# One out run per pair of heads, and half an out unit carried over a stage: attention followed by a two-layer snake network on one core

## The chip, the cores and the metric

The kernel runs on one core of a Trainium2 chip. The metric is the device time of one execution in microseconds (us). Each kernel has one profile. All runs here are with a mean granted TensorE clock of 0.985 to 0.996. Engines: PE is TensorE's matmul work, PEld its weight loads, ACT is ScalarE, DVE VectorE, POOL GpSimd.

## The reference, cut to what matters

```python
# 8 batches, 12 heads, 448 tokens, head size 64
q_n, k_n = rmsnorm(q, g_q), rmsnorm(k, g_k)
attn = softmax(q_n @ k_n.T / sqrt(64))
x = (attn @ v)            # per batch 448 x 768
h = x @ w_in              # 768 -> 2048, the "first product"
g = h + sin(alpha * h) ** 2 / (alpha + 1e-9)
out = g @ w_out           # 2048 -> 768, the "second product" or "out work"
```

## The kernel before

The program is a row of stages on TensorE: attention of batch 0, first product of batch 0, then for each batch b from 1 to 7 an attention stage followed by a first product. The second product of batch b-1 is cut into small steps of two matmuls each, called fillers, that are dealt out between the score and value matmuls of the attention of batch b. They give TensorE work while ACT computes exponentials. The second product of batch 7 stands alone at the end.

448 tokens are three tiles of 128 and a rest of 64. So even batches have three out units of 128 tokens, and odd batches have four: the fourth joins the rest of the even batch before and the first 64 tokens of the odd one. A unit has 16 steps (batch 0 has half units of 8 steps, because the second half of `w_out` lands late: in the trace it is issued at 47.4 us, the two halves take 26.6 and 29.2 us from issue to landing, and the first out matmul starts at 66.5). An attention stage therefore holds 48 or 64 steps, in turn.

```python
psum = ctx.enter_context(tc.tile_pool(name="ps", bufs=4, space=bass.MemoryType.PSUM))  # 4 slots, each a bank_pair
...
def scores(pi, t, warm=0):          # one tile of 128 keys, two heads
    sc = bank_pair("sc")
    ...                             # two matmuls, each on 64 rows of the array
    nc.scalar.activation(expT[pi][:, 2 * t:2 * t + 2, :], sc[:, :, :S], ACT.Exp, scale=SCALE)
...
units = [(i, (0, 1)) for i in range(NT + odd)] if b else [(i, (h,)) for h in range(2) for i in range(NT)]
if b == B - 1:
    units[-1:] = [(NT + odd - 1, (h,)) for h in range(2)]
...
for b in range(1, B):
    fillers.extend(second_product(b - 1))
    n_fill = len(fillers)
    ...
    step_of(ci, 5)()                # rsqrt of the norm for pairs 4 and 5: two small ACT instructions
    ...
    for p in range(NP):             # six pairs of heads
        ...                         # quota: 16 steps for pair 0, the rest spread evenly; part = its quarters
        if p == 0 and b > 1:
            fill(part[2])
        scores(pi, 0)
        scores(pi, 1)
        if p:
            attend(pi - 1)          # av: 16 value matmuls, then logarithm, exponential, multiply
        else:
            fill(part[3] - (part[2] if b > 1 else 0))
        if p % 2 == 0:
            rest_scores(pi)         # the rest keys of two pairs
        beside_e(4 * p)             # norm of the next batch; holds an rsqrt on ACT in pairs 2 and 4
        if p:
            fill(part[2])
            beside_e(4 * p + 1)
            scores(pi, 2)
            fill(part[3] - part[2])
        else:
            beside_e(4 * p + 1)
            scores(pi, 2)
        beside_e(4 * p + 2)
        fill(part[4] - part[3])
        beside_e(4 * p + 3)
    fill(len(fillers))
    attend(b * NP + NP - 1)
    ...
    first_product(b, beside_h(b))
```

Of the kernel before, what the change touches and what calls it, by code (L numbers as in the profile page):

```python
# [32 lines left out]
def kernel(  # L33
# [21 lines left out]
    B, H, S, D = q.shape  # L55
# [4 lines left out]
    MT = D_FF // P  # L60
    NP = H // 2
    NT = S // P
# [24 lines left out]
    def bank_pair(name):  # L87
        return psum.tile([P, 2, 512], F32, tag="ps", name=name)
# [3 lines left out]
    def load_qk(ci, k_queue=nc.sync):  # L92

        b, dp = ci // NC, ci % NC
        qk[ci] = inp.tile([P, 2, 2 * NJ, D], F32, tag="qk", name="qk")
        for which, src, queue in ((0, q, nc.sync), (1, k, k_queue)):
            heads = src[b].rearrange("(hi dp pp) (p j) d -> dp (pp p) hi (j d)", hi=2, pp=2, j=NJ)[dp]
            queue.dma_start(out=qk[ci][:, which].rearrange("p (hi j) d -> p hi (j d)", hi=2), in_=heads)

    def rest_rows(pi, hi):  # L100

        r = (hi + pi) % 2
        return slice(r * 64, r * 64 + 64)

    def load_v(b):


        vb[b] = vpool.tile([P, NT * H + NP, D], BF16, tag="vb", name="vb")
        parts = []
        tok = v[b].rearrange("h (p j) d -> p h (j d)", j=NJ)  # L110
        for jj in range(2):
            parts.append((vb[b][jj * 64:jj * 64 + 64, :NT * H, :].rearrange("p (h t) d -> p h (t d)", t=NT),
                          tok[:, :, jj * NT * D:(jj + 1) * NT * D]))
        last = v[b].rearrange("(hi dp pp) (p j) d -> j hi pp p dp d", hi=2, pp=2, j=NJ)[NJ - 1]
        slots = vb[b][:, NT * H:, :].rearrange("p (dp pp) d -> pp p dp d", pp=2)
        for hi in range(2):
            for pp in range(2):
                parts.append((slots[pp][rest_rows(pp, hi)], last[hi, pp]))
        return [lambda o=o, i=i: nc.gpsimd.dma_start(out=o, in_=i) for o, i in parts]  # L119
# [147 lines left out]
    def scores(pi, t, warm=0):  # L267

        sc = bank_pair("sc")
        for _ in range(warm):  # L270
            nc.tensor.matmul(sc[:, 0], blank[:, :P], blank, start=True, stop=True)
        qt, kt = qkT[pi][:, 0, :], qkT[pi][:, 1, :]
        if pi not in expT:
            expT[pi] = epool.tile([P, 2 * NT + 1, S], BF16, tag="expT", name="expT")
        for hi in range(2):
            r = slice(hi * 64, hi * 64 + 64)
            nc.tensor.matmul(sc[:, hi, :S], kt[r, t * P:(t + 1) * P], qt[r, :], start=True, stop=True)  # L277
        nc.scalar.activation(expT[pi][:, 2 * t:2 * t + 2, :], sc[:, :, :S], ACT.Exp, scale=SCALE)  # L278

    def rest_scores(pi):  # L280

        sc = bank_pair("sc3")
        for pp in range(2):
            if pi + pp not in expT:
                expT[pi + pp] = epool.tile([P, 2 * NT + 1, S], BF16, tag="expT", name="expT")
            for hi in range(2):
                r = slice(hi * 64, hi * 64 + 64)
                nc.tensor.matmul(sc[rest_rows(pp, hi), pp, :S], qkT[pi + pp][r, 1, NT * P:S], qkT[pi + pp][r, 0, :],
                                 start=True, stop=True)
        for pp in range(2):  # L290
            nc.scalar.activation(expT[pi + pp][:, 2 * NT, :], sc[:, pp, :S], ACT.Exp, scale=SCALE)  # L291
# [72 lines left out]
    def second_product(b):  # L364


        steps = []
        odd = b % 2
        rows = [out[c * S:(c + 1) * S, :].rearrange("(p j) d -> j p d", j=NJ) for c in range(B)]
        units = [(i, (0, 1)) for i in range(NT + odd)] if b else [(i, (h,)) for h in range(2) for i in range(NT)]  # L370
        if b == B - 1:
            units[-1:] = [(NT + odd - 1, (h,)) for h in range(2)]
        for i, halves in units:
            st = {}

            def step(m, i=i, halves=halves, st=st):
                if m == 0:
                    st["ps"] = bank_pair("ops")
                c0 = odd * (S + REST) + i * P if i < NT else NT * P
                lhsT = g_sb[:, m, c0:c0 + P]  # L380
                for k, half in enumerate(halves):
                    nc.tensor.matmul(st["ps"][:, k, :HALF], lhsT, w_out_sb[:, m, half * HALF:(half + 1) * HALF],  # L382
                                     start=(m == 0), stop=(m == MT - 1))
                if m == MT - 1:
                    n = len(halves)
                    osb = opool.tile([P, 2, HALF], F32, tag="osb", name="osb")
                    nc.vector.tensor_copy(osb[:, :n], st["ps"][:, :n, :HALF])  # L387
                    o = osb[:, :n].rearrange("p a d -> p (a d)")
                    cols = slice(halves[0] * HALF, (halves[-1] + 1) * HALF)
                    for jj in range(2):  # L390
                        dst = rows[b][odd + 2 * i + jj] if i < NT else rows[b - 1 + jj][(NJ - 1) * (1 - jj)]
                        eng = nc.scalar if b == B - 1 and jj else nc.sync
                        eng.dma_start(out=dst[:, cols], in_=o[jj * 64:jj * 64 + 64, :])
            each = 2 // len(halves)
            steps += [lambda m=m, s=step, e=each: [s(m * e + x) for x in range(e)] for m in range(MT // each)]
        return steps

    fillers = deque()

    def fill(n):  # L400
        for _ in range(min(n, len(fillers))):
            fillers.popleft()()
# [29 lines left out]
    def begin_norm(ci):  # L432
        norm[ci] = norm_tasks(ci)
        if ci + 2 < NC * B and ci != NC + 2:
            load_qk(ci + 2)

    def step_of(ci, *steps):
        return lambda: [norm[ci].steps[n]() for n in steps]

    def beside_h(b):  # L440

        ci = NC * b + 5
        if ci >= NC * B:
            return {}
        return {0: [lambda: begin_norm(ci)], 1: [step_of(ci, 0)], 3: [step_of(ci, 1)], 4: [step_of(ci, 3)],
                5: [step_of(ci, 2)], 7: [step_of(ci, 4)]}

    FIRST = 16
    for p in range(NP):
        scores(p, 0, BUSY[2 + p])  # L450
        scores(p, 1)
# [39 lines left out]

    for b in range(1, B):
        nc.scalar.preload_act_table_set(EXP_LN)
        fillers.extend(second_product(b - 1))
        n_fill = len(fillers)

        at = [[] for _ in range(4 * NP + 8)]
        s0, ci = 2, NC * b + 2
        if b == 1:
            load_qk(ci + 2)  # L500
        step_of(ci, 5)()
        at[s0].append(step_of(ci, 6))
        if b + 1 < B:
            for ci in (NC * b + 3, NC * b + 4):
                at[s0] += [lambda ci=ci: begin_norm(ci), step_of(ci, 0, 1, 2)]
                for n, step in ((4, 3), (5, 4), (6, 5), (8, 6)):
                    at[s0 + n].append(step_of(ci, step))
                s0 += 8
            for n, part in enumerate(load_v(b + 1)):
                at[s0 - 1 + n].append(part)  # L510

        def beside_e(slot):
            for task in at[slot]:
                task()

        for p in range(NP):
            pi = b * NP + p
            if p == 0:
                quota = min(FIRST, n_fill)
            else:  # L520
                left = max(n_fill - FIRST, 0)
                quota = left * p // (NP - 1) - left * (p - 1) // (NP - 1)
            part = [quota * j // 4 for j in range(5)]
# [5 lines that stand above are left out]
                attend(pi - 1)  # L529
            else:  # L530
                fill(part[3] - (part[2] if b > 1 else 0))
            if p % 2 == 0:
                rest_scores(pi)
            beside_e(4 * p)
            if p:
                fill(part[2])
                beside_e(4 * p + 1)
                scores(pi, 2)
                fill(part[3] - part[2])
            else:  # L540
                beside_e(4 * p + 1)
                scores(pi, 2)
            beside_e(4 * p + 2)
            fill(part[4] - part[3])
            beside_e(4 * p + 3)
        fill(len(fillers))
        attend(b * NP + NP - 1)
        for slot in range(4 * NP, len(at)):
            beside_e(slot)
        first_product(b, beside_h(b))  # L550
# [30 lines left out]
```

## Time and profile before

| | before |
|---|---|
| median of four runs | 465.85 us (465.0 to 466.45) |
| span of the profiled run | 463.9 us |
| PE / ACT / POOL / DVE busy | 441.4 / 344.2 / 293.3 / 227.2 us |
| attention stage with 64 steps (batches 2, 4, 6) | 37.60 us |
| attention stage with 48 steps (batches 3, 5) | 33.12 us |
| the same, batch 1 and batch 7 | 34.43 and 32.46 us |
| first product, each | 18.28 us |

A stage's length is read from the chain of waits, where each first product shows as one piece of 96 matmuls: the start of the next piece less the start of this one, less 18.28. Three of these pieces (start, duration; 155.31 - 99.43 - 18.28 = 37.60, and 206.71 - 155.31 - 18.28 = 33.12):

```profile
99.43 18.28 PE hps L341 x96
155.31 18.28 PE hps L341 x96
206.71 18.28 PE hps L341 x96
```

### The profile page before, as it was taken

What the parts mean: (1) busy time and instruction counts of PE and PEld (TensorE: products, weight loads), DVE (VectorE), ACT (ScalarE), POOL (GpSimd) and SP (SyncE); (2) the same over time, 40 slices, a digit from 0 to 9 for tenths busy, and PEclk for the clock granted to TensorE, in tenths of its full rate; (3) what the DMA queues carried; (4) which work ended last, traced back from release to release, by engine and by line L of the source; (5) the groups of instructions that cost most, each with busy time, mean ns of one, the idle gap of its engine ahead of it and who ended that gap; (6) DMA issues with size and microseconds to landing.
All of it is one profiled execution on the core that took longest, in us unless ns stands there. A gap on an engine that the chain in (4) does not pass through costs nothing.

```text
span 463.9 us, 7776 instructions
## 1 busy us (share of the span) xinstructions
PE 441.4 (95%) x2956; PEld 213.7 (46%) x2956; DVE 227.2 (49%) x331; ACT 344.2 (74%) x555; POOL 293.3 (63%) x299
## 2 busy tenths in 40 slices
PE   7678999999999999999999999999999999999996
PEld 2323544445444454445444454445544455445563
DVE  3775474526444365544654264454734356224521
ACT  4869788868977588877877588877887678986800
POOL 3977967868767387786667577795677666101400
PEclk9989999999999999999999999999999999999999
DMA  6999998485055911679065930559043760211023
GB/s 238 189 243 240 217 165 241 139 95 133 13 176 154 159 55 43 144 170 166 0 154 154 135 112 1 155 157 210 1 134 93 99 70 2 74 35 35 0 52 85
DMA packets 81353, 54.98 MB, mean 119 GB/s; under 512 B 60052, under 2 KB 77476, under 8 KB 81316
## 3 DMA queue, kind: packets, MB, share of 16 engines
q1 hardware_dynamic: 56210, 40.97, 35.0%
q0 software_dynamic: 24160, 11.81, 20.8%
q10 hardware_dynamic: 946, 1.70, 1.0%
q8 instruction: 23, 0.38, 0.4%
q14 instruction: 14, 0.11, 0.1%
HBM read 45.62 MB, written 11.01 MB: 122 GB/s over the span
## 4 chain that ended last, share of the span: by engine, by line
PE 74%; ACT 14%; issue 3%; DVE 3%; DMA 3%; POOL 2%; SPq 0%; DVEq 0%; POOLq 0%
PE hps L341 32%; PE ops L382 21%; PE av L310 16%; ACT expT L278 5%; PE sc L277 4%; ACT expT L291 3%; ACT rec L313 2%; ACT rec L312 2%; DMA vb<-in_v_dram 2%; DVE ms L208 1%; POOL s L325 1%; DMA g_rows<-in_g_q_dram 1%; DVE osb L387 1%; ACT inv L215 1%; ACT inv L216 1%
## 5 line engine op out<-in xcount | busy, mean ns | idle before, releaser
L382 PE MATMUL ops<-w_out_sb,g_sb 128*128 128x384 bf16 x896 | 161.5, 327 | 1.0 <-DVE g_sb L330 1.0
L278 ACT ACTIVATE expT<-sc 128x896 bf16<-128x896 f32 x144 | 125.4, 918 | 30.8 <-PE sc L277 30.5
L341 PE MATMUL hps<-xT,w_in_sb 128*128 128x448 bf16 x768 | 146.7, 353 | 0.0
L318 DVE TENSOR_TENSOR xT<-av,rec 64x448 bf16<-64x448 f32 x96 | 59.7, 622 | 117.3 <-ACT rec L313 116.5
L325 POOL TENSOR_TENSOR s<-s 128x448 f32<-128x448 f32 x64 | 59.4, 932 | 84.1 <-ACT s L322 71.4
L382 PEld LDWEIGHTS <-g_sb 128*128 128x128 bf16 x896 | 80.8, 98 | 68.9 <-issue 21.2
L330 DVE SCALAR_TENSOR_TENSOR g_sb<-s,inv_alpha_sb,hps 128x448 bf16<-128x448 f32 x128 | 81.2, 677 | 63.3 <-POOL s L325 58.1
L341 PEld LDWEIGHTS <-w_in_sb 128*128 128x128 bf16 x768 | 74.5, 98 | 70.3 <-issue 1.6
L322 ACT ACTIVATE s<-hps,alpha_sb 128x448 f32<-128x448 f32 x128 | 74.7, 628 | 28.4 <-PE hps L341 26.8
L310 PE MATMUL av<-expT,vb 128*64 128x448 bf16 (+1 forms) x384 | 71.4, 364 | 7.0 <-ACT expT L278 4.0
L202 POOL TENSOR_TENSOR sq<-qk 128x896 f32<-128x896 f32 x42 | 70.1, 1683 | 6.0 <-DVE ms L208 3.2
L226 POOL TENSOR_TENSOR qkn<-qk,inv 128x448 bf16<-128x448 f32 x42 | 38.5, 938 | 49.2 <-issue 32.0
L310 PE MATMUL av<-expT,ones 128*64 128x448 bf16 (+1 forms) x384 | 67.6, 358 | 0.0
L205 POOL TENSOR_TENSOR qk<-qk,gg 128x896 f32<-128x896 f32 x24 | 50.2, 2093 | 3.9 <-ACT gg L155 3.6
L277 PE MATMUL sc<-qkT 64*128 64x448 bf16 x288 | 44.7, 358 | 4.0 <-ACT expT L291 2.0
L387 DVE COPY osb<-ops 128x768 f32<-128x768 f32 (+1 forms) x32 | 27.4, 858 | 40.7 <-PE ops L382 40.4
L310 PEld LDWEIGHTS <-vb 128*64 128x64 bf16 (+1 forms) x384 | 23.8, 108 | 47.9 <-issue 41.1
L208 DVE TENSOR_REDUCE ms<-sq 128x14 f32<-128x896 f32 x42 | 44.8, 1081 | 1.6 <-POOL sq L202 0.8
L312 ACT ACTIVATE rec<-av 128x448 f32<-128x448 f32 x48 | 26.1, 545 | 20.9 <-PE av L310 18.6
L327 ACT ACTIVATE s<-s 128x448 f32<-128x448 f32 x64 | 36.9, 577 | 2.9
L228 POOL TENSOR_TENSOR qkn<-qk,inv 128x384 bf16<-128x384 f32 x42 | 34.0, 831 | 0.0
L119 POOL DMA_DIRECT2D vb<-in_v_dram x48 | 32.1, 686 | 0.0
(50 smaller groups left out, 197.2 us busy)
## 6 DMA issues: line engine op xcount, KB each, us to landing
qk<-in_q_dram SPq DMA_DIRECT2D x24, 448.0 KB, 5.6
qk<-in_k_dram SPq DMA_DIRECT2D x22, 448.0 KB, 7.0
out_dram<-osb SPq DMA_DIRECT2D x45, 192.0 KB, 4.5
vb<-in_v_dram POOLq DMA_DIRECT2D x16, 288.0 KB, 8.0
w_in_sb<-in_moe_w_in_dram POOLq DMA_DIRECT2D x2, 1536.0 KB, 17.4
w_out_sb<-in_moe_w_out_dram POOLq DMA_DIRECT2D x2, 1536.0 KB, 27.9
out_dram<-osb SPq DMA_DIRECT2D x14, 96.0 KB, 4.4
qk<-in_k_dram ACTq DMA_DIRECT2D x2, 448.0 KB, 6.0
```

The lines of the kernel that those rows point to most:

```text
L202: nc.gpsimd.tensor_mul(st.sq[w], qk[ci][:, w], qk[ci][:, w])
L205: eng.tensor_mul(qk[ci][:, 0], qk[ci][:, 0], gg.to_broadcast([P, 2 * NJ, D]))
L208: nc.vector.reduce_sum(st.ms[:, w, :], st.sq[w], axis=AX.X)
L277: nc.tensor.matmul(sc[:, hi, :S], kt[r, t * P:(t + 1) * P], qt[r, :], start=True, stop=True)
L278: nc.scalar.activation(expT[pi][:, 2 * t:2 * t + 2, :], sc[:, :, :S], ACT.Exp, scale=SCALE)
L310: nc.tensor.matmul(av[o, part, :S], lhsT, rhs, start=(t == 0), stop=(t == NT))
L318: nc.vector.tensor_mul(xT[b][r, hp, :], av[r, 0, :S], rec[o, :])
L322: nc.scalar.activation(s1, hps, ACT.Sin, scale=alpha_sb[:, m, :])
L325: nc.gpsimd.tensor_mul(s2, s1, s1)
L330: nc.vector.scalar_tensor_tensor(g_sb[:, m, (b % 2) * S:(b % 2 + 1) * S], s2, inv_alpha_sb[:, m, :], hps, op0=ALU.mult, op1=ALU.add)
L341: nc.tensor.matmul(ps[:, m % 2, :S], w_in_sb[:, kt, m * P:(m + 1) * P], x[:, kt, :], start=(kt == 0), stop=(kt == KT - 1))
L382: nc.tensor.matmul(st["ps"][:, k, :HALF], lhsT, w_out_sb[:, m, half * HALF:(half + 1) * HALF], start=(m == 0), stop=(m == MT - 1))
```

## The change

The intent is twofold. The third score tile of a pair moves ahead of its out work, so that the out work is one run and not two. And half a unit (8 steps) of each odd batch stays in the queue over the next first product and is done at the end of the attention stage after it, so that 64 and 48 become 56 and 56. For that the joined unit of an odd batch comes first (it reads columns of the even batch that the next first product overwrites), and its last unit is split in two halves.

```diff
-        units = [(i, (0, 1)) for i in range(NT + odd)] if b else [(i, (h,)) for h in range(2) for i in range(NT)]
-        if b == B - 1:
-            units[-1:] = [(NT + odd - 1, (h,)) for h in range(2)]
+        order = [NT] * odd + list(range(NT))
+        units = [(i, (0, 1)) for i in order] if b else [(i, (h,)) for h in range(2) for i in order]
+        if odd:
+            units[-1:] = [(NT - 1, (h,)) for h in range(2)]
...
-    FIRST = 16
+    FIRST, KEPT = 16, MT // 2
...
-        fillers.extend(second_product(b - 1))
-        n_fill = len(fillers)
+        fillers.extendleft(reversed(second_product(b - 1)))
+
+        n_fill = len(fillers) - (KEPT if b % 2 == 0 else 0)
...
+            scores(pi, 2)
             beside_e(4 * p)
             if p:
                 fill(part[2])
                 beside_e(4 * p + 1)
-                scores(pi, 2)
                 fill(part[3] - part[2])
             else:
                 beside_e(4 * p + 1)
-                scores(pi, 2)
             beside_e(4 * p + 2)
             fill(part[4] - part[3])
             beside_e(4 * p + 3)
-        fill(len(fillers))
         attend(b * NP + NP - 1)
```

## The prediction

The stages come to -7.55 us, so 458.3 from 465.82, put at 458.8. What the sum rests on is in the trace of the kernel before: 0.10 to 0.11 us at each change of shape (from 128\*64 to 64\*64, for one, the step from 131.55 to 131.84 is 0.29 for a pass of 0.19) and 0.1626 us an out matmul (20.81 us for 128). "Shape of the array" means, here and below, the pair that the profile prints with each matmul, such as 64\*128. The lengths of the new stages and the times within a pair in step 2 are estimates from the runs and durations of that trace.

> **What bounds the kernel now.** I read the page first, then busy time by stage, then the chain of waits, then TensorE's timeline inside two attention stages, then its waits stage by stage.
>
> ```profile
> span 463.9 us, 7776 instructions
> PE 441.4 (95%) x2956; PEld 213.7 (46%) x2956; DVE 227.2 (49%) x331; ACT 344.2 (74%) x555; POOL 293.3 (63%) x299
> PE 74%; ACT 14%; issue 3%; DVE 3%; DMA 3%; POOL 2%; SPq 0%; DVEq 0%; POOLq 0%
> ```
>
> TensorE is busy 95% of the span and holds 74% of the chain that ended last. No matmul is added or removed, so only two things can shrink: its 22.5 us of idleness (463.9 - 441.4), and time hidden inside "busy" that does no useful work.
>
> The stages, from the chain: the first product of each batch is a solid 18.28 us, the seven attention stages lie between, and the last second product closes. Those attention stages, with the time from one first product to the next less 18.28, take 34.43 (batch 1), 37.60, 33.12, 37.60, 33.12, 37.60 and 32.46 us, in sum 245.93. Batches 2, 4, 6 carry 64 out steps, the others 48. The windows of batches 2 and 3:
>
> ```profile
> 117.70:155.30 37.60, 37.06 (x273) 17.46 (x272) 17.84 (x23) 28.04 (x44) 26.95 (x29) 1.00 0.48 118
> 173.60:206.70 33.10, 31.98 (x241) 14.85 (x240) 16.79 (x22) 27.71 (x44) 25.95 (x28) 1.00 0.48 114
> ```
>
> The columns are window, length, then busy time of PE, PEld, DVE, ACT, POOL. ACT does the same 28 us in both. The full stage leaves TensorE 0.54 us idle, the thin one 1.12. Where the thin one loses it:
>
> ```profile
> PE av L310 <- ACT expT L278: 0.7, 3, 0.3
> PE av L310 <- DVE osb L387: 0.3, 1, 0.3
> ```
>
> Three times attention-times-V waits for the third exponential of its pair; once it waits for the PSUM slot of an out unit that ended in the middle of a pair. The full stage has one of the former (0.2) and one scores wait (0.2).
>
> The hidden time shows in TensorE's timeline of one pair with 64 steps (start, duration, operation):
>
> ```profile
> 132.05 0.36 PE L288 MATMUL sc<-qkT 64*64 64x448 bf16 x4
> 132.34 1.80 PE L382 MATMUL ops<-w_out_sb,g_sb 128*128 128x384 bf16 x10
> 134.07 0.36 PE L277 MATMUL sc<-qkT 64*128 64x448 bf16 x2
> 134.37 1.80 PE L382 MATMUL ops<-w_out_sb,g_sb 128*128 128x384 bf16 x10
> 136.10 0.55 PE L277 MATMUL sc<-qkT 64*128 64x448 bf16 x4
> ```
>
> Ten out matmuls take 1.73 us from start to next start; eight take 1.41 elsewhere in this stage; the closing product runs 128 in 20.81, so 0.1626 each. Both runs are therefore longer by 0.11 than their matmuls. The two score matmuls, which use different row halves, take 0.30 where one pass of 448 columns takes 0.19 (18.28 / 96): again 0.11. So every change of the array's shape costs about 0.11 us, counted as busy.
>
> [...]0.11 us at each change between 128x128, 64x128, 128x64 and 64x64, none inside a run. [...] In the trace the two rsqrt instructions queued ahead of the third exponential (189.08 and 189.43, then 189.56) delay it just before a wait at 190.51.
>
> **The change part by part.**
>
> 1. The third score tile moves ahead of the out work, so pairs 1 to 5 have one out run, not two. The order was: scores, av, (rest scores), out, scores, out. It becomes: scores, av, (rest scores), scores, out. One change of shape goes per pair; the change from rest scores or av to the third scores stays (0.32 - 0.19 for rest to third in the first stage, 70.64 to 70.96, so again about 0.11). 5 pairs x 7 stages x 0.11 = 3.8 us off TensorE's path.
>
> 2. The third exponential is issued 1.1 to 1.7 us earlier and ahead of rsqrt. With 16 out matmuls behind it, the next av comes about 3.2 us after the third scores (16 x 0.1626 + 0.11 + 0.48 for the next scores). ACT per even pair, counted from its first scores: first exponential starts at 0.40, second ends at 2.13, logarithm and reciprocal exponential to 3.3, two rest exponentials to 4.1, third to 5.0, rsqrt to 5.5. The next av starts at 5.25 + 0.48 = 5.7. The waits in thin stages should go: 0.8 in each of batches 3 and 5, 0.3 in batch 7.
>
> 3. Units of 16 steps now end at pair ends, with quotas of 8: FIRST takes unit one, pairs 1-2 and 3-4 one each, pair 5 the half. The slot of a finished unit is then wanted third or fourth in the next pair, some 2 us after its end, and the copy takes 0.96. The 0.3 waits on the copy go.
>
> 4. The sum of steps stays 384; batches 2 to 7 get 56. Moving 8 steps (16 x 0.1626 = 2.6 us) from a full to a thin stage is by itself zero.
>
> 5. Added: three half copies and six more output transfers of 96 KB in place of three copies of 0.96 us and six transfers of 192. A half copy takes 0.56. DVE is 49% busy; nothing on the path. The closing product only changes order and still ends in a half unit.
>
> Now the stages. A stage of 64, pair by pair: 6.61 (pair 0, unchanged), 5.78, 6.00, 5.49, 6.27, 5.81, last av 1.57. To 56 steps with one run: pair 1 loses two matmuls and a switch (5.35), pair 2 four and a switch (5.24), pair 3 two and a switch (5.06), pair 4 as pair 2 plus a wait of 0.27 (5.24), pair 5 four and a switch (5.05). Sum 34.12, called 34.3 with 0.2 for new small waits. Then:
> - batches 2, 4, 6: 37.60 to 34.3, 3 x -3.3 = -9.9
> - batches 3, 5: 33.12 to 34.3, 2 x +1.2 = +2.4
> - batch 7 (no next batch to normalise): 32.46 to 34.1, +1.65
> - batch 1: keeps 48 steps, keeps the 1.0 wait for the last snake output, loses 5 switches (0.55) and the waits of 0.85 and 0.45 of its scores: about -1.7
> In all -7.55, so 458.3 from 465.82. I put 458.8, since not every wait will vanish.
>
> **Rivals.** *The PSUM slot becomes the wait.* While an out unit is held only three slots rotate: first scores, second scores, av, rest scores in the first slot, third scores in the second. In an even pair the third scores start at 0.48 + 1.47 + 0.29 = 2.24 us and need the second exponential, done at 2.13: almost no room. Likewise the next second or first scores may need the av slot, free at about 2.0 + 1.15 + 1.26 = 4.4 against 5.2. Pair 0 already shows such a wait (rest to third scores 0.49 where 0.32 is free of it). At 0.1 to 0.3 in two pairs of seven stages this costs 1.5 to 4 us: 460 to 462.
>
> *ACT becomes the bound in even pairs.* 5.5 us of ACT with rsqrt against 5.25 of TensorE; odd pairs have 3.6 against 5.06 and take up the excess, and per stage it is 28 against 34. In batch 1, with 12 matmuls per pair, ACT runs 0.9 late into the next pair. If it spills into av waits: about 461. Rsqrt now waits behind the third exponential, so POOL's scaling and the square sums on DVE come 1 us later and could hold up DVE's multiply in pair 4.
>
> *Only levelling pays, and switches do not.* If the 0.11 belonged to each operation's first weights and not to the change of shape, part 1 would give nothing: 465.8 - 3.7 = 462. Against it: the gap is absent at 64x64 av to 64x64 rest scores (0.21 for one pass of 0.19).
>
> **Range and chances.** The low end takes all of part 1, all waits and no new one, with a little more from pair 0: 457.2. The high end is the slot rival: 461.8. Over 2% means below 456.5, which needs about 1.8 us beyond the whole sum: 0.06. Slower by 2% would need a deadlock-like stall in each pair: 0.01.
>
> **What would show it.** One run of 16 out matmuls per pair, 2.71 us from start to next start, with scores straight before it; stages of batches 2 to 7 within 0.3 us of each other near 34.3; TensorE's busy time down by 3.5 to 4; no av wait on the third exponential after pair 0 and none on the output copy. Wrong if stages stay above 35, if third scores wait for exponentials in pairs 2 and 4, or if busy time does not fall.

## The result, and the profile after

The changed kernel takes 458.47 us in the median of four runs (457.84 to 459.44), against 465.85 (465.0 to 466.45). The ratio is 0.9845, with a 95% interval of 0.9819 to 0.9871. Ratios are computed as the mean time of one kernel's runs over that of the other's of the same rounds, so they are not quite the ratio of the medians quoted. The result is thus inside 2%, and clear of noise.

The first lines of the page of the changed kernel, and its chain by engine:

```profile
span 456.9 us, 7795 instructions
PE 436.8 (96%) x2952; PEld 215.0 (47%) x2956; DVE 227.9 (50%) x334; ACT 341.6 (75%) x555; POOL 293.1 (64%) x299
...
PE 81%; ACT 8%; issue 3%; DMA 3%; DVE 2%; POOL 2%; SPq 0%; DVEq 0%; POOLq 0%
```

The span fell by 7.0 us and PE's busy time by 4.6 (by 4.2 within the seven attention stages, 239.14 to 234.96), although no matmul was removed, and TensorE holds more of the chain than before (74%). The stages of batches 1, 2 and 3, by busy time of each engine (window, length, PE, PEld, DVE, ACT, POOL, clock, DMA share, GB/s):

```profile
65.00:98.70 33.70, 31.81 (x241) 14.72 (x238) 17.35 (x25) 27.65 (x44) 24.86 (x26) 1.00 0.68 167
116.90:151.10 34.20, 33.86 (x258) 16.18 (x256) 17.44 (x23) 27.59 (x44) 25.57 (x27) 1.00 0.39 105
169.40:203.60 34.20, 33.86 (x258) 16.20 (x256) 17.44 (x23) 27.59 (x44) 25.57 (x27) 1.00 0.43 106
```

The second and third are now alike, 34.20 us with 0.34 idle, and so are all six stages of batches 2 to 7. Their lengths come from these pieces of the chain (151.15 - 98.67 - 18.28 = 34.20):

```profile
98.67 18.28 PE hps L341 x96
151.15 18.28 PE hps L341 x96
203.63 18.28 PE hps L341 x96
```

Batch 1, which still has 48 steps, leaves PE 1.9 us idle. One pair on TensorE's timeline:

```profile
125.91 0.36 PE L277 MATMUL sc<-qkT 64*128 64x448 bf16 x2
126.20 2.77 PE L383 MATMUL ops<-w_out_sb,g_sb 128*128 128x384 bf16 x16
128.91 0.55 PE L277 MATMUL sc<-qkT 64*128 64x448 bf16 x4
```

Scores stand straight before one run of 16 out matmuls, 2.71 us from its start to the next start. What TensorE still waits for in a stage of batches 2 to 7 (batch 2; total us, times, longest):

```profile
PE av L310 <- ACT expT L278: 0.2, 1, 0.2
```

It is the wait of the first av for the third exponential of pair 0. In batch 1 two waits are left:

```profile
PE ops L383 <- DVE g_sb L330: 1.0, 1, 1.0
PE ops L383 <- ACT expT L291: 0.9, 1, 0.9
```

Adding up the stages: batches 2, 4, 6 went from 37.60 to 34.20 (3 x -3.40), batches 3 and 5 from 33.12 to 34.20 (2 x +1.08), batch 7 from 32.46 to 34.20 (+1.74), batch 1 from 34.43 to 33.70 (-0.73). The sum is -7.03, the whole fall of the span.

### The profile page after: what moved, and what is told of

Read it like the earlier page. It is cut to its first block, busy times and chain, and to the rows that moved or that the text cites. A ratio compares the mean times of both kernels' runs of the same rounds, so it can differ in the third digit from the quotient of the medians.

```text
span 456.9 us, 7795 instructions
## 1 busy us (share of the span) xinstructions
PE 436.8 (96%) x2952; PEld 215.0 (47%) x2956; DVE 227.9 (50%) x334; ACT 341.6 (75%) x555; POOL 293.1 (64%) x299
## 4 chain that ended last, share of the span: by engine, by line
PE 81%; ACT 8%; issue 3%; DMA 3%; DVE 2%; POOL 2%; SPq 0%; DVEq 0%; POOLq 0%
PE hps L341 32%; PE ops L383 26%; PE av L310 16%; PE sc L277 6%; ACT expT L278 4%; DMA vb<-in_v_dram 2%; ACT expT L291 2%; DVE ms L208 1%; POOL s L325 1%; DMA g_rows<-in_g_q_dram 1%; ACT rec L313 1%; ACT rec L312 1%; PE sc L288 1%; ACT inv L215 1%; DVE g_sb L330 0%
## 5 line engine op out<-in xcount | busy, mean ns | idle before, releaser
L383 PE MATMUL ops<-w_out_sb,g_sb 128*128 128x384 bf16 x896 | 155.6, 327 | 1.9 <-DVE g_sb L330 1.0
L383 PEld LDWEIGHTS <-g_sb 128*128 128x128 bf16 x896 | 83.6, 98 | 65.3 <-issue 13.1
L310 PEld LDWEIGHTS <-vb 128*64 128x64 bf16 (+1 forms) x384 | 22.8, 108 | 46.5 <-issue 39.4
```

The costliest lines, as they stand in the source:

```text
L310: nc.tensor.matmul(av[o, part, :S], lhsT, rhs, start=(t == 0), stop=(t == NT))
L383: nc.tensor.matmul(st["ps"][:, k, :HALF], lhsT, w_out_sb[:, m, half * HALF:(half + 1) * HALF], start=(m == 0), stop=(m == MT - 1))
```

## The experiments

Seven kernels ran, each five rounds against the kernel before; all gave correct results. Of each I quote the stage of batches 2 to 7 beside the time, because the start's spread (up to 1.9 us) goes into the time. Ratios are to the kernel before; the runs were taken on two chips and in other rounds than the main comparison, so times of two experiments are compared by their stages first.

### The run alone

```diff
 (the kernel before)
             if p % 2 == 0:
                 rest_scores(pi)
+            scores(pi, 2)
             beside_e(4 * p)
             ...                     # and the two later scores(pi, 2) taken out
```

> The third score tile is moved ahead of the out work, but the stages keep 48 and 64 steps. My theory (each change of the array's shape costs 0.11 us, and one fewer goes per pair in 35 pairs): TensorE busy down by about 4 us, full stages near 36.8 us, thin ones near 31.7, time 459 to 460, since units that end inside a run may cost a few waits of 0.4 to 0.9 for a PSUM slot. Rival (only the levelling to 56 steps pays): no less than 464.

It took 462.47 us (461.46 to 463.21), ratio 0.9927 (0.9908 to 0.9945). That is between the two expectations: half the gain, 3 us short of my number. PE's busy time fell to 437.3 (in the stage of batch 2 from 37.06 to 36.62), as the theory has it. The full stages fell from 37.60 to 37.19 and the thin ones from 33.12 to 32.58, though five changes of shape at 0.11 should have brought 0.54 and the waits something on top. The waits in a thin stage (batch 3):

```profile
PE av L310 <- DVE osb L387: 0.6, 1, 0.6
PE av L310 <- ACT expT L278: 0.2, 1, 0.2
PE sc L277 <- DVE xT L318: 0.2, 1, 0.2
```

The waits for the third exponential in pairs 3 and 5 are gone; only pair 0's is left. In their place stand waits for PSUM slots: av of the next pair takes the slot of the out unit that ended after four of the seven steps of pair 3's run, and waits until DVE has copied it. The full stages have a like wait, of a unit that starts in the middle of a run (batch 2, pair 4):

```profile
142.04 1.48 PE L382 MATMUL ops<-w_out_sb,g_sb 128*128 128x384 bf16 x8
143.74 2.11 PE L382 MATMUL ops<-w_out_sb,g_sb 128*128 128x384 bf16 x12 [0.23 <-ACT expT L291]
145.79 0.55 PE L277 MATMUL sc<-qkT 64*128 64x448 bf16 x4
```

The new unit needs a slot that the rest exponentials still hold, and the run of 20 matmuls takes 3.75 us (142.04 to 145.79) where the run of 20 in pair 2 takes 3.36. (From start to start the waits of this run cost 0.08 to 0.17 us more than the view lists: 0.39 against 0.23 here, 0.65 against 0.57 and 0.34 against 0.17 in batch 3. The view counts from modelled ends.) So part of the gain of the whole change belongs to the carrying.

### The carrying alone

```diff
 (the changed kernel, its pair in the old order)
-            scores(pi, 2)
             beside_e(4 * p)
             if p:
                 fill(part[2])
                 beside_e(4 * p + 1)
+                scores(pi, 2)
                 fill(part[3] - part[2])
             else:
                 beside_e(4 * p + 1)
+                scores(pi, 2)
```

> Stages hold 56 steps, the half unit is carried, but the out work of a pair stays in two runs around the third scores. Theory: each of the six stages is 34.2 + 5 x 0.11 = 34.7 us, the waits of the thin stages are gone, the switches are not: about 462.8. Rival (levelling does all): 458.5 to 459.5. Rival (levelling does nothing): 465.8.

It took 462.69 us (461.76 to 463.61), ratio 0.9938 (0.9917 to 0.9958). Two first products that follow each other on the chain:

```profile
151.21 18.28 PE hps L341 x96
204.22 18.28 PE hps L341 x96
```

204.22 - 151.21 - 18.28 gives a stage of 34.73 us, 0.53 over the changed kernel's 34.20, against 5 x 0.11 = 0.55. TensorE's only wait in it is again the 0.2 of pair 0. Over the six stages of batches 2 to 7 the sums are 211.5 us before, 208.8 with the run alone, 208.4 with the carrying alone, 205.2 with both. The parts bring 2.7 and 3.1, which is 5.8 of the 6.3 that both bring together, so they nearly add.

### Two more changes of shape

```diff
 (the changed kernel)
             scores(pi, 0)
+            if p:
+                fill(part[2])
             scores(pi, 1)
             if p:
                 attend(pi - 1)
             ...
             if p:
-                fill(part[2])
                 beside_e(4 * p + 1)
                 fill(part[3] - part[2])
```

> The changed kernel with the first half of each pair's out run put between the first and the second score tile: the same matmuls, two more changes of shape per pair in 35 pairs. Theory: 70 x 0.11 = 7.5 us more, counted as TensorE busy and not as waits: near 466, stages of 35.3. If the 0.11 us were not the change of shape, or were hidden, it stays near 458.5.

It took 469.64 us (469.31 to 471.16), ratio 1.0091 (1.0072 to 1.011): slower than the kernel before, and 3.6 us more than I expected. A stage of batch 2, and the part of its pair 1 that was split:

```profile
118.14:153.93 35.79, 35.10 (x257) 16.32 (x256) 17.44 (x23) 27.92 (x44) 24.89 (x26) 1.00 0.35 100
```

```profile
124.74 0.36 PE L277 MATMUL sc<-qkT 64*128 64x448 bf16 x2
125.04 1.47 PE L383 MATMUL ops<-w_out_sb,g_sb 128*128 128x384 bf16 x8
126.44 0.36 PE L277 MATMUL sc<-qkT 64*128 64x448 bf16 x2
...
128.31 0.36 PE L277 MATMUL sc<-qkT 64*128 64x448 bf16 x2
128.60 1.48 PE L383 MATMUL ops<-w_out_sb,g_sb 128*128 128x384 bf16 x8
130.01 0.36 PE L277 MATMUL sc<-qkT 64*128 64x448 bf16 x2
```

Pair 1, which waits for nothing, takes 130.01 - 124.74 = 5.27 us. The same matmuls without the split take 5.05 in a pair without a wait (139.21 less 134.16 in the changed kernel). The 0.22 for two changes of shape is what the theory says, and it is in the busy column: 35.10 in the stage of batch 2 where the changed kernel has 33.86, with ten changes more. PE's total rose from 436.8 to 444.7, 7.9 us for 70 changes (70 x 0.11 is 7.7; the expectation rounded it down to 7.5). Most of the miss is a wait that the edit made: in pairs 3 and 5 scores wait for rest exponentials, 0.23 each time, a slot wait that the later second scores may have brought about by pushing ACT back (not shown); all over the program these waits rose from 0.6 to 3.3 us. So the size of the cost is settled, with a side cost that is not its own.

This edit also adds changes of operation, so it can't tell the one from the other. The changed kernel's trace can, where av ends and the rest scores of the next pair follow:

```profile
130.66 0.38 PE L310 MATMUL av<-expT,ones 64*64 64x448 bf16 x2
130.86 0.36 PE L288 MATMUL sc<-qkT 64*64 64x448 bf16 x4
131.16 0.36 PE L277 MATMUL sc<-qkT 64*128 64x448 bf16 x2
```

Between two operations of one shape (64*64) the step is 0.20 us, a bare pass of 0.19; from there to the shape 64*128 it is 0.30. So the 0.11 goes with the shape and not with the operation.

A second control lies in the changed kernel's batch 1: there a run of 14 out matmuls from 85.02 to 87.40 holds the end of one half unit and the start of the next. 2.38 us is 14 x 0.1626 plus 0.10: a new unit with a new slot inside a run, without a new shape, costs nothing here.

### 56 steps, but units that end inside runs

```diff
 (the changed kernel)
                 quota = left * p // (NP - 1) - left * (p - 1) // (NP - 1)
+                if b > 1:
+                    quota = (0, 7, 10, 7, 10, 6)[p]
```

> The changed kernel, still 56 steps per stage and one run per pair, but pairs 1 to 5 of batches 2 to 7 take 7, 10, 7, 10 and 6 steps in place of 8 each, so that two units of a stage end one or two steps before the end of a run. If the level of 56 alone brought what carrying brings, the stages stay at 34.2 us and the time near 458.5. If it is that units end where runs end, the waits of av for the copy of a finished unit come back (0.3 to 0.6, once or twice a stage): stages of 34.6 to 35.2, time 461 to 464.

It took 459.58 us (459.43 to 459.73), ratio 0.9869 (0.9852 to 0.9887). Its stages are 34.51 us, 0.31 over the aligned ones: neither expectation was met, since the stages did not stay at 34.2 and fell just short of the lower edge of the second, 34.6. One of the two units of a stage brought a wait (waits of batch 2):

```profile
PE av L310 <- DVE osb L388: 0.2, 1, 0.2
PE av L310 <- ACT expT L278: 0.2, 1, 0.2
```

So these unit ends cost 6 x 0.31 = 1.9 us of the 3.6 us (208.8 - 205.2) that carrying adds to the single run. With these quotas the unit that ends one step before the end of the run costs a wait, and the one that ends two steps before does not. In batch 2 the copy of the first (133.03, 0.97 long) ends at 134.00, after the av's turn at 133.73 (0.48 after the scores). The copy of the second ends near 144.62, an estimate from the first, whose copy ended 1.08 after its last matmul (133.25 less two of 0.1626): just before the av starts at 144.67.

The traces of the run alone show where all of the 3.6 us lies. Read from start to start, its slot waits are worth 0.39 in each full stage (above), 0.99 in each thin one (0.65 for the av that waits for the copy, 0.34 for the scores behind it) and 0.45 in batch 7: 3 x 0.39 + 2 x 0.99 + 0.45 = 3.6. Without them the stages would be 36.80, 31.59 and 31.59, which is 34.20 with the 2.60 of 8 steps added or taken off, to 0.01. So the level of 56 brings nothing by itself; what carrying saves are slot waits. Whether 48 and 64 steps dealt so that units end at run ends would do as well (48 as 16, 8, 8, 5, 5, 6, for example) was not run.

### Rsqrt ahead of the third exponential

```diff
 (the changed kernel)
-            scores(pi, 2)
             beside_e(4 * p)
+            scores(pi, 2)
```

> The changed kernel with rsqrt queued on ACT ahead of the third exponential again, as before the change. Theory: with 16 out matmuls in one run behind the third scores, the exponential ends at 5.5 us of the pair and is wanted at 5.7, so stages stay at 34.2 to 34.4 and the time at 458 to 460. If the order on ACT is what removed the waits: av waits of about 0.25 in pairs 3 and 5, six stages of 34.7, time 461 to 462.

It took 459.6 us (458.22 to 460.07), ratio 0.9865 (0.9843 to 0.9888). The stages of batches 2 to 7 are 34.20 us, exactly those of the changed kernel. ACT does the two rsqrt instructions first, in pair 2 of batch 2:

```profile
133.14 0.32 ACT L215 ACTIVATE inv<-ms,eps 128x28 f32<-128x28 f32 x1
133.49 0.23 ACT L216 ACTIVATE inv<-inv 128x28 f32<-128x28 f32 x1
133.62 0.90 ACT L278 ACTIVATE expT<-sc 128x896 bf16<-128x896 f32 x1
```

The third exponential ends at 134.52, and the scores of the next pair start at 134.31, with the av that needs it 0.48 later. The exponential is ready 0.27 us before it is wanted. In the changed kernel, without the rsqrt ahead of it, it ends at 133.91 for an av at 134.64: 0.73 to spare, which buys nothing. Only batch 1, with 12 to 14 matmuls behind the scores, became longer: 34.18 against 33.70.

### Rsqrt of pair 0 behind its exponentials

The wait that is left in every stage is ACT's: after the first product it still has snake work, then the load of the exponential table (1.28 us), then rsqrt (0.55 us), and only then the first exponential.

```diff
 (the changed kernel)
-        step_of(ci, 5)()
+        at[0].append(step_of(ci, 5))    # run by beside_e(0), after scores(pi, 2) of pair 0
```

> The changed kernel with the two rsqrt instructions of pair 0 queued on ACT behind pair 0's third exponential instead of ahead of its first. Theory: what is left of TensorE's waits in a stage (0.2 for the third scores of pair 0, 0.23 for the first av) is ACT being 0.55 us late, so each of six stages loses up to 0.43: about 456, stages of 33.8. Rival: POOL's scaling starts 2 us later, [...] the gain is lost or turned into a new wait for the av slot: 458 to 461.

It took 456.81 us (455.29 to 457.21), ratio 0.9802 (0.978 to 0.9824). The stages of batches 2 to 7 are 33.73 us, 0.47 less. The rival did happen in its first half: POOL's scaling started 4.7 us after the stage's first scores in place of 1.7, and DVE waited 1.62 us for the square sums that follow it, but DVE's multiplies came in time: no wait of TensorE names them in batches 2 to 7. Batch 1 became 0.37 longer, and there the rival did show: scores of pair 3 wait 0.2 for the slot that DVE's multiply sets free.

```diff
 (the same)
+        if b == 1:
+            step_of(ci, 5)()
+        else:
+            at[0].append(step_of(ci, 5))
```

> As the run with rsqrt of pair 0 late, but batch 1 keeps it early. There the late rsqrt made the stage 0.37 us longer (34.07 against 33.70) and the other six 0.47 shorter. Expected: stages of 33.73 and 33.70, about 2.8 us under the changed kernel, 455.5 to 456.5. If batch 1's stage is longer for another reason (its first scores, the DMA of the start), no gain over the run before: 456.8.

It took 455.49 us (454.86 to 456.08), ratio 0.9782 (0.9762 to 0.9802): 3.0 us under the changed kernel by the medians, of which 6 x 0.47 = 2.8 are the stages. The 1.3 us to the run before are more than batch 1 can give (0.37); the start, 1.9 us earlier in this profile, may be in them. Batch 1 itself is back where it was: from its first out matmul to the next first product it takes 32.06 us, as in the run with unaligned units, which starts as early and has the changed kernel's batch 1. Among profiles with the later start it was 32.60 with rsqrt late and 32.22 in the changed kernel. This version beats both kernels; whether it is over 2% faster than the first is not settled, since the interval ends at 0.9802. Its batch 2:

```profile
115.65:149.37 33.72, 33.72 (x257) 15.92 (x256) 17.53 (x23) 27.60 (x44) 25.59 (x27) 1.00 0.40 108
```

PE is busy for the whole of the stage, and no wait is listed in it. What these traces still show to take from such a stage is its changes of shape.

## Why the prediction was right or wrong

The prediction was 458.8 us with 457.2 to 461.8; measured were 458.47. By its steps:

1. *One change of shape fewer per pair, 3.8 us.* Right. Carrying alone against both differs by 0.53 us per stage, where 0.55 was worked out, and two more changes per pair put 7.9 us into PE's busy time. The rival that switches do not pay falls with this. The fall of busy time was put at 3.5 to 4 and was 4.6 over the whole program, where the two traces hold 2956 and 2952 matmul records, and 4.2 within the seven stages.

2. *The third exponential earlier and ahead of rsqrt; the waits of thin stages go.* The waits went, and the single run alone removes those for the exponential. The order against rsqrt was credited too much: with 16 out matmuls in the run it is worth nothing in batches 2 to 7, as the estimate of 5.5 against 5.7 in the same step implied. The timing itself was right: the third exponential ended at 5.00 of pair 2 in batch 2, rsqrt at 5.47, and the next av came at 5.73 (5.0, 5.5 and 5.7 predicted).

3. *Units end at pair ends, the waits for the copy go.* Right, and worth more than the prediction gave it: it counted 0.3 per thin stage. Without the carrying the longer single run makes these waits 0.6, and shifting the quotas at 56 steps brings 0.31 per stage back. That is why the single run alone missed my expectation by 3 us.

4. *Moving 8 steps is by itself zero.* Not run by itself, but the stages of the run alone bear it out to 0.01 us once their slot waits are taken off.

5. *Copies and transfers: nothing on the path.* DVE's busy time rose by 0.7 us and no wait in batches 2 to 7 names them.

*The stages.* 34.12 was worked out pair by pair and called 34.3; it is 34.20, so the margin of 0.2 for new waits was too wide by 0.1 in six stages. Batch 1 was the mis-sized term: about -1.7 predicted, -0.73 measured. Its wait of 0.85 for a slot of rest scores did not vanish. The third scores no longer needed that slot, but the next half unit did, in the middle of pair 2's run, and waited 0.88 for the same rest exponentials. The rival "the PSUM slot becomes the wait" therefore came true in this one place, where units end inside runs, and in none of the stages for which it was argued. The two errors have opposite signs: about 0.4 us better in batches 2 to 7 than predicted (-6.30 against -5.85), about 1.0 worse in batch 1. The sum of the stages was -7.55 on paper and -7.03 on the chip. That 458.8 came within 0.3 us of 458.47 is partly luck: the errors cancel in part, 0.5 us was added for waits of which the 34.3 already held 0.2 a stage, and four runs of the changed kernel spread over 1.6 us. What the runs support are the stages, to 0.1 us in six of seven.

*ACT becomes the bound in even pairs.* It did not, but it is close: the stages' last waits were ACT's, in pair 0, and taking 0.55 us of ACT work out of the way there brought 0.47 us.

What stays open: why the granted clock was 0.79 between 28 and 36 us in the two main profiles, and why the matmuls there are slow in four profiles and not in the other five, which no run looked into; and whether aligned units at 48 and 64 steps would be as fast.

## What to carry to other kernels

When TensorE is busy nearly all the time (95% here) and no matmul can go, count the changes of the array's shape on its timeline: a run's length from start to next start, less its matmuls at the pace of a long run, is what each change costs (0.11 us here). When work is dealt out as filler, let its units end where the runs end, so that the slot of a finished unit is not the next one wanted (units ending inside runs cost 0.31 us a stage here). After a stage has been evened out, look at its first pair: what a slower engine still owes from the stage before is paid there, and moving a small instruction behind the urgent ones can remove it (0.47 us a stage here).
